# A fused attention and SoLU kernel: buffers named one by one, and a new order table

## The chip, the cores and the metric

The kernel runs on one core of a Trainium2 chip. The metric is the device time of one execution in microseconds (us). A core has five engines with queues of their own: TensorE (PE, matmuls), VectorE (DVE), ScalarE (ACT), GpSimd (POOL) and SyncE (SP). Each takes its instructions in the order of its queue. SP, ACT and POOL also issue DMA transfers.

## What is computed

```python
# q, k, v: (8, 8, 576, 64); x: (4608, 512); w_in: (512, 1024); w_out: (1024, 512)
kv = einsum('bhsd,bhse->bhde', k, v)
out = einsum('bhsd,bhde->bhse', q, kv)
out = out / sqrt(mean(out * out, -1) + 1e-6) * g_norm
x = out.transpose(0, 2, 1, 3).reshape(B * S, H * D)
h = x @ w_in
e = exp(h - max(h))
solu = h * e / (sum(e) + 1e-9)
ln = (solu - mean(solu)) / sqrt(var(solu) + 1e-6) * g_ln
return ln @ w_out
```

## The kernel before, in words

The 4608 tokens are nine tiles of 512 (c = 0 to 8). Tiles 0 to 7 take the first 512 tokens of a batch each; tile 8 takes the last 64 of all eight batches, and its q lies in a buffer of its own, q_last.

A tile goes through these pieces; a piece's name is its kind and its indices.

- `k.b`, `v.b`, `q.b`, `q_last.b` (lines 300 to 317): loads of a batch, DMAs that POOL issues, with a cast to bf16. `w_in`, `w_out` are loads of the weights, POOL's too.
- `kv_mm.b` (365): PE forms k^T v. `kv.b.x.part` (378): DVE or ACT copies it from PSUM.
- q is transposed: for tiles 0 to 3 by PE (`qT_mm`, 400) with a copy (`qT`), for tiles 4 to 8 by one transposing DMA that SP issues (`qT.c`, 411).
- `o_mm` (417) is q times kv; `sq`, `s_mm` or `s_pair`, `ln`, `ex` (430 to 462) make the root mean square of each head; `x` and `xc` (464 to 477) scale into x.
- `h.c.f` (520) is x times w_in for 128 of the 1024 columns; `exp.c.f` (527, ACT) is e; `u.c.f` (531, DVE) is h times e. No maximum is taken off and nothing is divided here; both go into the row factor below.
- `usq.c.f` (535, POOL or ACT) squares u; `es.c.n` (539, POOL) adds two of the e.
- `sums.c` (559, PE) adds u, usq and es over the columns with 80 small matmuls, in that order. `turn`, `stats` (DVE) and `rstd` (ACT) make of them one factor per token.
- `out.c.m.part` (618, PE) is u times the centred w_out; `ob.c.m` (633) scales it by rstd, on DVE or ACT; `store.c.m` (637) writes 128 rows with two DMAs from SP (tile 8: one DMA).

**What sets the order.** A class `Plan` (107) holds all pieces with what they need and which buffers they use. A table of words, `ORDER`, lists all 880 pieces once; `emit` (135) walks it and issues each piece on its engine (a suffix such as `:act` picks another). So each engine's queue is the table cut down to that engine. A second table, `HOME`, tells for some PSUM buffers in which group of banks they lie. Waits between engines are put in by the framework from the data and the buffers.

**Buffers.** PSUM has eight banks in the groups h (2), out (2), o (2), s, misc. SBUF buffers of a kind are kept in a number of slots (188 to 191): three for each of k, v, q and qT, four for e and ob, two for u, usq, es, x and wf. In the kernel before, `bank` (196) and `kept_tile` (202) ask the framework's pool for a tile with the kind's tag and that number of buffers, and the framework picks the slot when it places the tile. `emit` only asserts that the piece which takes a slot in turn comes behind all users of the tile that had it in turn. A load into a slot waits for the last reader of what was there.

A DMA that POOL or SP issues also takes one of eight semaphores of its side in turn, so it waits until the DMA eight issues earlier has landed.

Names of buffers in the profile: `misc_ps` in L372 is kv, in L405 q transposed, in L566 the sums; `qT_sb`, `q_sb`, `usq_sb`, `es_sb`, `u_sb`, `e_sb` are the tiles above; `wf_sb` holds w_out in 32 bits and later the scaled rows of odd tiles, `ob_sb` those of even tiles.

Of the kernel before, what the change touches and what calls it, by code (L numbers as in the profile page):

```python
# [20 lines left out]
warm load1.v load1.k v.0.0 k.0.0 v.0.1 g_in cast1.v:act q.0.0 k.0.1 q.0.1 q.1.0 cast1.k:act ident k.1.0 v.1.0 turn_g  # L21
kv_mm.0.0 warm.0 warm.2 kv.0.0.2 kv.0.0.1:act warm.1 kv.0.0.0:act qT_mm.0.0 warm.3 g_mean qT.0.0:act o_mm.0.0
kv_mm.0.1 sq.0.0.0 kv.0.1.2:act kv.0.1.0:act sq.0.0.1 w_in.1 kv.0.1.1 qT_mm.0.1 s_mm.0.0.0 warm.6 w_in.0 q.1.1 v.1.1
qT.0.1 k.1.1 s_mm.0.0.1 ex.0.0.1 x.0.0.1 o_mm.0.1 qT_mm.1.0 sq.0.1.1 qT.1.0 warm.5 w_out.0 sq.0.1.0 ex.0.0.0 w_out.1
s_mm.0.1.0 ex.0.1.0 s_mm.0.1.1 kv_mm.1.0 x.0.0.0 v.2.0 warm.4 kv.1.0.1 kv.1.0.0 ex.0.1.1 kv.1.0.2:act x.0.1.0 o_mm.1.0
table sq.1.0.0 h.0.5.0 x.0.1.1 sq.1.0.1 h.0.6.0 h.0.5.1 h.0.7.0 s_mm.1.0.1 h.0.7.1 h.0.1.0 exp.0.5 ln.1.0.1 exp.0.7
s_mm.1.0.0 u.0.5 h.0.1.1 h.0.6.1 ex.1.0.1 x.1.0.1 u.0.7 h.0.0.0 ln.1.0.0 qT_mm.1.1 h.0.3.0 qT.1.1 h.0.0.1 exp.0.1
h.0.2.0 h.0.3.1 kv_mm.1.1 ex.1.0.0 u.0.1 exp.0.6 h.0.2.1 exp.0.0 k.2.0 q.2.0 usq.0.7 q.3.0 exp.0.3 kv.1.1.2:act
kv.1.1.0:act exp.0.2 x.1.0.0 u.0.0 kv.1.1.1 o_mm.1.1 sq.1.1.1 h.0.4.0 u.0.6 h.1.0.0 s_mm.1.1.1 u.0.3 es.0.0 sq.1.1.0
u.0.2 ln.1.1.1 h.0.4.1 s_mm.1.1.0 ln.1.1.0 ex.1.1.0 ex.1.1.1 es.0.3 w_mean.0 x.1.1.0 h.1.5.0 es.0.1 v.3.0 usq.0.5  # L30
x.1.1.1 exp.0.4 es.0.2 w_mean.1 usq.0.1 usq.0.0:act u.0.4 h.1.2.0 w_center.4 h.1.6.0 h.1.0.1 usq.0.3:act w_center.2
exp.1.0 h.1.6.1 h.1.5.1 h.1.2.1 h.1.1.0 exp.1.6 exp.1.5 u.1.0 w_center.0 exp.1.2 u.1.5 k.3.0 h.1.7.0 h.1.1.1 u.1.6
k.4.0 exp.1.1 h.1.7.1 h.1.4.0 kv_mm.2.0 h.1.3.0 exp.1.7 kv.2.1.0:act kv.2.1.2:act kv.2.0.0:act kv.2.1.1:act h.1.4.1
q.4.0 v.4.0 usq.0.2 w_center.1 u.1.7 u.1.1 es.1.0 w_center.3 w_center.5 w_center.7 out.0.0.0 q_last.2 usq.0.4:act
w_center.6 kv.2.0.1:act out.0.3.0 h.1.3.1 kv.2.0.2:act exp.1.4 qT_mm.2.0 u.1.2 out.0.3.1 qT.2.0:act out.0.0.1
qT_mm.2.1 out.0.0.2 u.1.4 qT.2.1 o_mm.2.0 usq.0.6:act sums.0 turn.0 stats.0 out.0.0.3 exp.1.3 u.1.3 usq.1.1 sq.2.0.1
sq.2.0.0 out.0.3.2 usq.1.7 out.0.1.0 v.5.0 usq.1.2:act rstd.0 s_pair.2.0 ob.0.0 usq.1.0 k.5.0 ln.2.0.1 out.0.3.3
out.0.2.0 qT_mm.3.1 ob.0.3 ln.2.0.0 ex.2.0.1 o_mm.2.1 out.0.2.1 qT.3.1 sq.2.1.1 sq.2.1.0 es.1.3 usq.1.3 out.0.1.1
xc.2.0.1.0 out.0.2.2 xc.2.0.1.1 ex.2.0.0 usq.1.4 es.1.2 s_pair.2.1 out.0.1.2 ln.2.1.0 ln.2.1.1 store.0.0 out.0.2.3
out.0.1.3 ex.2.1.0 x.2.0.0 ob.0.2 ex.2.1.1 h.2.3.0 kv_mm.3.0 q.5.0 es.1.1 usq.1.5 ob.0.1:act store.0.3 qT.4 h.2.1.0  # L40
x.2.1.0 xc.2.1.1.1 store.0.2 kv.3.0.0:act h.2.7.0 h.2.6.0 h.2.0.0 xc.2.1.1.0 kv.3.1.1:act kv.3.1.2:act h.2.1.1 h.2.3.1
h.2.0.1 kv.3.0.1 kv.3.0.2 exp.2.1 qT_mm.3.0 h.2.7.1 kv.3.1.0 u.2.1 usq.1.6:act exp.2.3 exp.2.7 h.2.6.1 exp.2.0 exp.2.6
qT.3.0 h.2.4.0 sums.1 u.2.3 u.2.7 turn.1 k.6.0 v.6.0 u.2.0 o_mm.3.0 sq.3.0.1 h.2.4.1 out.1.3.0 stats.1 sq.3.0.0
exp.2.4 s_pair.3.0 h.2.5.0 out.1.3.1 ln.3.0.0 ex.3.0.0 u.2.4 qT.5 h.2.5.1 rstd.1 exp.2.5 u.2.6 x.3.0.0 ob.1.3 es.2.0
usq.2.1 u.2.5 out.1.0.0 kv_mm.4.0 kv.4.1.1 ln.3.0.1 h.2.2.0 o_mm.3.1 ex.3.0.1 kv.4.1.2:act h.2.2.1 out.1.0.1 kv.4.1.0
sq.3.1.0 xc.3.0.1.1 xc.3.0.1.0 ob.1.0 kv.4.0.0 sq.3.1.1 s_pair.3.1 out.1.1.0 usq.2.7 out.1.2.0 exp.2.2 ln.3.1.1
ex.3.1.1 q.6.0 u.2.2 es.2.2 k.7.0 ln.3.1.0 es.2.1 xc.3.1.1.1 usq.2.0 es.2.3 xc.3.1.1.0 ex.3.1.0 x.3.1.0 out.1.1.1
kv.4.0.1:act kv_mm.5.0 out.1.2.1 kv.5.0.0:act kv.4.0.2:act ob.1.1 h.3.2.1 h.3.0.1 kv.5.1.1 kv.5.1.0 h.3.1.1 usq.2.3
kv.5.1.2 exp.3.2 usq.2.6 u.3.2 usq.2.2:act usq.2.4:act h.3.5.1 ob.1.2 h.3.4.1 o_mm.4.1 usq.2.5 exp.3.0 u.3.0 kv.5.0.1
exp.3.1 exp.3.5 sq.4.1.0 es.3.0 u.3.1 sums.2 o_mm.4.0 kv.5.0.2 u.3.5 turn.2 stats.2 out.2.2.0 sq.4.1.1 store.0.1  # L50
store.1.1 exp.3.4 u.3.4 sq.4.0.1 s_pair.4.1 sq.4.0.0 out.2.2.1 usq.3.2 ln.4.1.1 ln.4.1.0 s_pair.4.0 ex.4.1.1 usq.3.0
xc.4.1.1.1 xc.4.1.1.0 es.3.2 ln.4.0.1 ex.4.0.1 ex.4.1.0 ln.4.0.0 xc.4.0.1.1 xc.4.0.1.0 rstd.2 out.2.0.0 x.4.1.0
out.2.0.1 h.3.7.1 store.1.3 kv_mm.6.0 ex.4.0.0 ob.2.0 usq.3.4:act h.3.3.1 out.2.3.0 kv.6.1.1 x.4.0.0 ob.2.2 h.3.6.1
exp.3.7 exp.3.3 out.2.3.1 usq.3.1 es.3.1 u.3.3 o_mm.5.0 exp.3.6 usq.3.3:act sq.5.0.1 u.3.7 usq.3.7 h.4.2.1 out.2.1.0
q_last.7 es.3.3 sq.5.0.0 kv.6.0.0 ob.2.3 kv.6.1.2 kv.6.0.2 kv.6.1.0 kv.6.0.1 s_pair.5.0 u.3.6 out.2.1.1 store.1.0
usq.3.5:act exp.4.2 h.4.1.1 ln.5.0.1 h.4.0.1 usq.3.6 ln.5.0.0 ex.5.0.1 v.7.0 q_last.1 u.4.2 ex.5.0.0 ob.2.1 exp.4.0
exp.4.1 h.4.4.1 sums.3 qT.6 xc.5.0.1.0 x.5.0.0 xc.5.0.1.1 u.4.0 o_mm.5.1 turn.3 exp.4.4 u.4.1 q_last.5 store.1.2
q_last.3 usq.4.0 q_last.4 q_last.6 usq.4.2 h.4.3.1 u.4.4 stats.3 sq.5.1.0 sq.5.1.1 h.4.5.1 s_pair.5.1 out.3.1.0
store.2.2 exp.4.3 ln.5.1.1 exp.4.5 rstd.3 u.4.3 u.4.5 h.4.7.1 ex.5.1.1 ln.5.1.0 out.3.1.1 h.4.6.1 out.3.0.0 kv_mm.7.0
ex.5.1.0 xc.5.1.1.0 xc.5.1.1.1 x.5.1.0 exp.4.7 o_mm.6.0 ob.3.1:act out.3.2.0 out.3.0.1 kv.7.0.0 kv.7.1.2 u.4.7  # L60
kv.7.1.1 store.2.1 usq.4.4 store.2.3 es.4.2 es.4.0 store.2.0 sq.6.0.0 kv.7.1.0:act sq.6.0.1 es.4.1 exp.4.6 kv.7.0.2
ob.3.0 u.4.6 usq.4.1 s_pair.6.0 kv.7.0.1:act out.3.2.1 usq.4.7 ln.6.0.0 ex.6.0.0 ln.6.0.1 h.5.5.1 exp.5.5 ob.3.2
ex.6.0.1 usq.4.3 usq.4.5 q.7.0 out.3.3.0 x.6.0.0 o_mm.6.1 sq.6.1.1 out.3.3.1 h.5.1.1 sq.6.1.0 es.4.3 s_pair.6.1
xc.6.0.1.1 xc.6.0.1.0 ln.6.1.0 exp.5.1 h.5.3.1 ob.3.3 u.5.5 u.5.1 exp.5.3 ex.6.1.0 out.4.1.0 usq.5.5 u.5.3 h.5.7.1
h.5.0.1 exp.5.7 ln.6.1.1 exp.5.0 x.6.1.0 h.5.4.1 qT.7 usq.4.6 u.5.7 u.5.0 usq.5.7 q_last.0 exp.5.4 h.5.2.1 ex.6.1.1
h.5.6.1 out.4.3.0 exp.5.2 u.5.2 u.5.4 sums.4 exp.5.6 usq.5.0:act es.5.2 u.5.6 usq.5.3 o_mm.7.0 turn.4 es.5.0 out.4.3.1
xc.6.1.1.1 stats.4 out.4.2.0 sq.7.0.1 sq.7.0.0 usq.5.1:act s_pair.7.0 out.4.2.1 out.4.1.1 rstd.4 ln.7.0.0 xc.6.1.1.0
ob.4.3 ln.7.0.1 ob.4.2 h.6.0.1 ex.7.0.0 x.7.0.0 out.4.0.0 h.6.6.1 out.4.0.1 h.6.5.1 usq.5.2 exp.6.0 ex.7.0.1
ob.4.1:act usq.5.6 es.5.3 xc.7.0.1.0 xc.7.0.1.1 usq.5.4 ob.4.0:act exp.6.6 qT.8 o_mm.7.1 sq.7.1.0 h.6.4.1 es.5.1 u.6.0
exp.6.5 sq.7.1.1 sums.5 usq.6.0 u.6.6 exp.6.4 u.6.5 turn.5 s_pair.7.1 ln.7.1.0 h.6.7.1 store.3.3 store.3.2 store.4.3  # L70
ln.7.1.1 ex.7.1.0 u.6.4 stats.5 x.7.1.0 h.6.3.1 h.6.2.1 h.6.1.1 exp.6.7 u.6.7 exp.6.3 out.5.0.0 u.6.3 out.5.1.0
usq.6.6 ex.7.1.1 exp.6.2 xc.7.1.1.1 u.6.2 usq.6.5 usq.6.3 exp.6.1 xc.7.1.1.0 u.6.1 out.5.2.0 o_mm.8.0 out.5.2.1
out.5.0.1 usq.6.7:act usq.6.2 usq.6.1 es.6.3 sq.8.0.1 sq.8.0.0 rstd.5 usq.6.4 store.3.1 store.4.1 s_pair.8.0 ln.8.0.1
ob.5.2 ln.8.0.0 es.6.0 out.5.1.1 out.5.3.0 h.7.6.1 ob.5.1 h.7.7.1 ob.5.0:act ex.8.0.1 h.7.1.1 ex.8.0.0 es.6.1
xc.8.0.1.1 xc.8.0.1.0 x.8.0.0 out.5.3.1 ob.5.3 exp.7.7 exp.7.1 store.4.2 store.4.0 store.5.2 exp.7.6 u.7.6 h.7.5.1
# [624 lines left out]
```

## Time and profile before

| what | value |
|---|---|
| three runs | 199.25, 200.31, 200.31 us; median 200.31 |
| profiled execution | 199.36 us, of which 197.5 us are the span from first to last instruction |
| mean granted TensorE clock | 0.977 |
| PE busy | 178.4 us (90%), 2227 matmuls |
| ACT busy | 144.8 us (73%) |
| POOL busy | 127.2 us (64%) |
| DVE busy | 125.6 us (64%) |
| DMA | 30.00 MB in 35420 packets |

How to read it: a row of the timeline gives start, duration, engine, line, operation, tile written and read, and in brackets how long the engine sat idle before it and what ended that. The rows of 40 digits cut the span into slices of 4.94 us, busy time in tenths; PEclk is the granted clock in tenths. The windows view gives, for each stretch, its length and then the busy time and number of instructions of each engine, the granted clock, the DMA engines' share and rate. The chain of waits of this execution goes back from the last store through PE alone, with hardly a wait, as far as it is shown (148 us). The trace also gives the time at which each load landed.

### The profile page before, as it was taken

How to read it: one execution, taken by the hardware profiler on the slowest of the kernel's cores; microseconds unless marked ns; L12 is line 12 of the kernel's file. 1: busy time of each engine (PE TensorE's matmuls, PEld its weight loads, DVE VectorE, ACT ScalarE, POOL GpSimd, SP SyncE). 2: the span in 40 equal slices, each digit the busy share in tenths (PEclk: the TensorE clock that was granted, in tenths of full speed). 3: DMA queues.
4: the chain of work that ended last, by engine and by line, in shares of the span. 5: the costliest groups of instructions: out<-in, count | busy, mean ns of one | idle time of the engine just before them, and what ended most of it. 6: DMA issues, size and time to landing. Idle time of an engine off the chain costs nothing. (4 is left out here: it accounts for less than half of the span.)

```text
span 197.5 us, 5401 instructions
## 1 busy us (share of the span) xinstructions
PE 178.4 (90%) x2227; PEld 85.1 (43%) x2227; DVE 125.6 (64%) x247; ACT 144.8 (73%) x255; POOL 127.2 (64%) x136
## 2 busy tenths in 40 slices
PE   7668999999999998179999999999999999999990
...
PEclk9999999999999999859999999999999999999997
...
GB/s 157 177 205 206 206 389 229 207 209 209 235 218 199 158 172 221 246 244 133 10 60 114 234 7 84 129 63 209 145 80 29 188 3 0 65 201 3 23 242 165
DMA packets 35420, 30.00 MB, mean 152 GB/s; under 512 B 16316, under 2 KB 29636, under 8 KB 35396
## 3 DMA queue, kind: packets, MB, share of 16 engines
...
q10 hardware_dynamic: 576, 0.92, 1.3%
...
## 5 line engine op out<-in xcount | busy, mean ns | idle before, releaser
L620 PE MATMUL out_ps<-w_out_sb,u_sb 128*128 128x512 bf16 x288 | 70.1, 384 | 0.1
L522 PE MATMUL h_ps<-x_sb,w_in_sb 128*128 128x512 bf16 x288 | 69.3, 380 | 0.3 <-DVE x_sb L466 0.2
L216 POOL TENSOR_TENSOR usq_sb<-u_sb 128x512 bf16<-128x512 bf16 x50 | 51.2, 1038 | 14.7 <-DVE u_sb L533 14.5
L533 DVE TENSOR_TENSOR u_sb<-h_ps,e_sb 128x512 bf16<-128x512 f32 x72 | 47.4, 685 | 17.2 <-ACT e_sb L529 16.0
L541 POOL TENSOR_TENSOR es_sb<-e_sb 128x512 bf16<-128x512 f32 x36 | 45.5, 1274 | 19.2 <-ACT e_sb L529 14.2
L529 ACT ACTIVATE e_sb<-h_ps,zero_t 128x512 f32<-128x512 f32 x72 | 46.3, 689 | 15.3 <-PE h_ps L522 11.7
L522 PEld LDWEIGHTS <-w_in_sb 128*128 128x128 bf16 x288 | 26.8, 97 | 33.6 <-issue 4.2
L620 PEld LDWEIGHTS <-u_sb 128*128 128x128 bf16 x288 | 26.6, 98 | 33.6 <-issue 4.7
L214 ACT ACTIVATE osq_sb<-o_ps,zero_t 128x512 bf16<-128x512 f32 x36 | 23.2, 685 | 9.4 <-PE o_ps L424 9.2
L474 DVE SCALAR_TENSOR_TENSOR x_sb<-o_ps,g_cols,rst_sb 64x512 bf16<-64x512 f32 x28 | 21.0, 750 | 7.4 <-ACT rst_sb L454 6.9
L450 ACT ACTIVATE lss_sb<-s_ps,eps_t 128x512 f32<-128x512 f32 x32 | 21.0, 682 | 3.0 <-PE s_ps L443 2.9
L454 ACT ACTIVATE rst_sb<-lss_sb,zero_t 128x512 f32<-128x512 f32 x32 | 22.6, 722 | 0.4
L466 DVE SCALAR_TENSOR_TENSOR x_sb<-o_ps,g_cols,rst_sb 128x512 bf16<-128x512 f32 x22 | 16.3, 749 | 8.4 <-ACT rst_sb L454 6.5
L305 POOL DMA_DIRECT2D q_sb<-in_q_dram x10 | 7.6, 764 | 15.5 <-DMA qT_sb<-q_sb 13.1
L214 ACT ACTIVATE usq_sb<-u_sb,zero_t 128x512 bf16<-128x512 bf16 x22 | 15.1, 718 | 0.8 <-DVE u_sb L533 0.8
L566 PEld LDWEIGHTS <-stat_sel 128*32 128x32 bf16 x720 | 10.6, 99 | 9.9 <-issue 9.5
L222 DVE TENSOR_SCALAR wf_sb<-out_ps,rstd 128x512 f32<-128x512 f32 x13 | 9.7, 745 | 7.2 <-PE out_ps L620 4.7
L566 PE MATMUL misc_ps<-usq_sb,stat_sel 128*32 128x128 bf16 x288 | 6.2, 225 | 6.5 <-POOL usq_sb L216 6.5
L210 DVE CAST kvd<-misc_ps 64x128 bf16<-64x128 f32 (+1 forms) x15 | 4.3, 287 | 11.8 <-PE misc_ps L372 6.7
L222 DVE TENSOR_SCALAR ob_sb<-out_ps,rstd 128x512 f32<-128x512 f32 (+1 forms) x13 | 9.1, 727 | 2.3 <-ACT ob_sb L220 1.8
L573 DVE STREAM_TRANSPOSE misc_ps<-misc_ps 128x128 f32<-128x128 f32 x9 | 3.0, 328 | 11.4 <-PE misc_ps L566 10.4
L424 PE MATMUL o_ps<-qT_sb,kvd 64*64 64x256 bf16 (+1 forms) x192 | 8.7, 258 | 1.2 <-ACT qT_sb L210 0.7
...
## 6 DMA issues: line engine op xcount, KB each, us to landing
...
```

The costliest lines, as they stand in the source:

```text
L214: nc.scalar.activation(out=dst, in_=src, func=AF.Square, bias=zero_t[:, :])
L216: on[engine].tensor_tensor(out=dst, in0=src, in1=src, op=MUL)
L222: nc.vector.tensor_scalar_mul(out=dst, in0=src, scalar1=by)
L450: nc.scalar.activation(out=t[:, :], in_=T["s", i][:, :], func=AF.Ln, bias=eps_t[:, :])
L454: nc.scalar.activation(out=t.rearrange("p a b c -> p (a b c)"), in_=T["lss", i][:, :], func=AF.Exp, scale=-0.5, bias=zero_t[:, :])
L474: nc.vector.scalar_tensor_tensor(out=t[rows, 2 * hf:2 * hf + 2, 1], in0=T["o", c, hf, 1][rows, :, :, :], scalar=g_cols[rows, NF:NF + 1], i ...
L522: nc.tensor.matmul(bank(("h", c, f), [128, 512])[:, :], w_in_sb[:, dt, f * 128:(f + 1) * 128], T["x", c][:, dt].rearrange("p a b c -> p (a ...
L529: nc.scalar.activation(out=t[:, f % 2, :], in_=T["h", c, f][:, :], func=AF.Exp, bias=zero_t[:, :])
L533: nc.vector.tensor_tensor(out=t[:, f, :], in0=T["h", c, f][:, :], in1=T["e", c, f // 2][:, f % 2, :], op=MUL)
L541: on[engine].tensor_tensor(out=t[:, n, :], in0=e[:, 0, :], in1=e[:, 1, :], op=ADD)
L566: nc.tensor.matmul(t[32 * j:32 * j + 32, 0, :], stat_sel[:, i, :], cols, start=(part == 0 and n == 0), stop=(part == 2 and n == n_src - 1) ...
L620: nc.tensor.matmul(bank(("out", c, m), [128, d_model])[:, :], T["u", c][:, f, m * 128:(m + 1) * 128], w_out_sb[:, f, :], start=(f == 0), s ...
```

## The change

Three things change, and nothing else: no piece is added or left out.

1. **Slots.** Every slot is a tag of its own (`q0`, `q1`, `q2`), and `emit` picks it: a free list per kind, filled when the last user of a tile has been issued, and taken from at the front. So a new tile takes the slot whose last user stands earliest in the table.
2. **ORDER** is another order of the same 880 pieces, and some pieces change engine (25 instead of 22 of the kv copies on ACT, 21 instead of 22 of the usq, 13 instead of 11 of the scalings).
3. **HOME** is another table of PSUM groups.

```diff
     def __init__(self, slots):
-        self.pieces, self.users, self.slots, self.homes = {}, {}, slots, {}
+        self.pieces, self.users, self.slots, self.homes, self.place = {}, {}, slots, {}, {}
...
-        done, held = set(), {tag: [] for tag in self.slots}
+        done, left = set(), {key: len(names) for key, names in self.users.items()}
+        free = {tag: ["%s%d" % (tag, i) for i in range(n)] for tag, n in self.slots.items()}
...
             for key in uses:
-                tag = self.home(key)
-                if key not in held[tag]:
-                    held[tag].append(key)
-                    if len(held[tag]) > self.slots[tag]:
-                        old = held[tag][-1 - self.slots[tag]]
-                        assert done.issuperset(self.users[old]), (name, old)
+                if key not in self.place:
+                    self.place[key] = free[self.home(key)].pop(0)
+                left[key] -= 1
+            for key in uses:
+                if not left[key]:
+                    free[self.home(key)].append(self.place[key])
...
-            tag = plan.home(key)
-            T[key] = ps.tile(shape, dtype, name=key[0] + "_ps", tag=tag, bufs=banks[tag])
+            T[key] = ps.tile(shape, dtype, name=key[0] + "_ps", tag=plan.place[key])
...
-            T[key] = sb.tile(shape, dtype, name=key[0] + "_sb", tag=key[0], bufs=kept[key[0]])
+            T[key] = sb.tile(shape, dtype, name=key[0] + "_sb", tag=plan.place[key])
```

Of the order, POOL's part between the sums of tiles 0 and 3 (loads of k, v, q and q_last among the es and usq pieces), the table before:

```
usq.1.1 usq.1.7 v.5.0 usq.1.0 k.5.0 es.1.3 usq.1.3 usq.1.4 es.1.2 q.5.0 es.1.1 usq.1.5 k.6.0 v.6.0
es.2.0 usq.2.1 usq.2.7 q.6.0 es.2.2 k.7.0 es.2.1 usq.2.0 es.2.3 usq.2.3 usq.2.6 usq.2.5
es.3.0 [sums.2] usq.3.2 usq.3.0 es.3.2 usq.3.1 es.3.1 usq.3.7 q_last.7 es.3.3 usq.3.6 v.7.0 q_last.1 [sums.3]
```

and after:

```
es.1.3 k.5.0 usq.1.1 usq.1.0 usq.1.7 q.5.0 es.1.1 es.1.0 es.1.2 usq.1.3 usq.1.4 usq.1.2
usq.2.0 es.2.0 usq.2.1 es.2.2 q_last.4 es.2.3 q_last.2 usq.2.6 es.2.1 usq.2.4 usq.2.7 usq.2.3
v.6.0 [sums.2] k.6.0 es.3.0 usq.3.5 q.6.0 es.3.2 usq.3.0 usq.3.2 usq.3.1 q_last.0 usq.3.4 q_last.6 es.3.1
usq.3.6 v.7.0 es.3.3 usq.3.3 [sums.3] k.7.0 q_last.1 usq.4.0 q_last.3 q_last.7 q_last.5 usq.4.1 q.7.0
```

On SP, qT.4 stands behind two stores of tile 0 in the table before and ahead of all stores after; the stores of tiles 0 to 2 stand later among the transposes. At the end, sums.8 stands ahead of nine parts of out before and of five after.

More of the change, by code (lines that the diff above doesn't have):

```diff
@@ L20 @@
 ORDER = """
[L21 to L75, printed above, removed]
@@ L76 @@
-h.7.0.1 h.7.3.1 es.6.2 exp.7.3 h.7.4.1 es.7.3 u.7.1 u.7.7 sums.6 u.7.3 exp.7.0 exp.7.4 exp.7.5 o_mm.8.1 u.7.5 h.7.2.1
-sq.8.1.1 exp.7.2 store.3.0 sq.8.1.0 u.7.4 turn.6 out.6.2.0 out.6.3.0 stats.6 s_pair.8.1 u.7.2 u.7.0 out.6.1.0
-usq.7.1:act ln.8.1.1 ln.8.1.0 out.6.3.1 store.5.0 es.7.0 usq.7.5 es.7.2 out.6.1.1 usq.7.6 usq.7.7 usq.7.3 ex.8.1.0
-ex.8.1.1 out.6.0.0 store.5.1 x.8.1.0 out.6.2.1 xc.8.1.1.1 xc.8.1.1.0 rstd.6 out.6.0.1 h.8.2.1 ob.6.1:act h.8.4.1
-ob.6.3 ob.6.2 h.8.3.1 h.8.0.1 usq.7.2 ob.6.0 exp.8.3 h.8.6.1 exp.8.2 exp.8.4 es.7.1 h.8.1.1 u.8.3 exp.8.6 u.8.2 u.8.4
@@ L81 @@
-usq.8.2:act h.8.5.1 exp.8.0 exp.8.1 h.8.7.1 exp.8.5 u.8.0 exp.8.7 es.8.1 out.7.1.0 out.7.2.0 u.8.1 store.6.2 u.8.5
-u.8.6 store.6.1 store.5.3 usq.8.6:act usq.8.1:act out.7.0.0 es.8.0 out.7.2.1 out.7.1.1 es.8.2 usq.8.4 usq.8.3:act
-usq.7.4:act usq.8.5 u.8.7 usq.8.0 out.8.2.0 usq.7.0:act out.7.0.1 store.6.3 sums.7 usq.8.7:act es.8.3 sums.8 turn.7
-stats.7 rstd.7 store.6.0 ob.7.2 turn.8 out.8.2.1 out.8.3.0 ob.7.0:act out.7.3.0 ob.7.1 store.7.0 stats.8 store.7.2
-store.7.1 out.8.1.0 out.8.0.0 out.8.1.1 rstd.8 ob.8.2:act store.8.2:act out.7.3.1 ob.7.3 out.8.0.1 ob.8.1:act
@@ L86 @@
-out.8.3.1 store.8.1:act store.7.3 ob.8.0:act store.8.0:act ob.8.3.1:act ob.8.3.0 store.8.3.0 store.8.3.1:act
+warm load1.k load1.v g_in k.0.0 v.0.0 v.0.1 cast1.v q.0.0 k.0.1 q.0.1 q.1.0 ident turn_g warm.0 cast1.k:act k.1.0
+kv_mm.0.0 kv.0.0.2:act warm.2 qT_mm.0.0 v.1.0 warm.3 g_mean kv.0.0.0:act kv_mm.0.1 kv.0.0.1:act qT.0.0:act o_mm.0.0
+kv.0.1.0:act w_in.1 w_in.0 q.1.1 v.1.1 k.1.1 qT_mm.0.1 sq.0.0.0 sq.0.0.1 w_out.0 kv.0.1.1 kv.0.1.2 qT.0.1 s_mm.0.0.0
+warm.6 s_mm.0.0.1 ex.0.0.0 ex.0.0.1 o_mm.0.1 qT_mm.1.0 sq.0.1.1 warm.5 x.0.0.0 sq.0.1.0 qT.1.0 s_mm.0.1.0 s_mm.0.1.1
@@ new lines @@
+x.0.0.1 warm.4 w_out.1 v.2.0 k.2.0 kv_mm.1.0 ex.0.1.1 ex.0.1.0 kv.1.0.2:act kv.1.0.1 warm.1 kv.1.0.0 table o_mm.1.0
+h.0.5.0 x.0.1.0 x.0.1.1 sq.1.0.0 h.0.6.0 h.0.5.1 h.0.7.0 sq.1.0.1 exp.0.5 s_mm.1.0.1 ln.1.0.1 h.0.7.1 s_mm.1.0.0
+h.0.1.0 h.0.6.1 u.0.5 h.0.0.0 h.0.1.1 ln.1.0.0 h.0.0.1 ex.1.0.1 q.2.0 usq.0.5 x.1.0.1 v.3.0 q.3.0 exp.0.7 u.0.7
+ex.1.0.0 h.0.3.0 qT_mm.1.1 h.0.3.1 h.0.2.0 kv_mm.1.1 x.1.0.0 exp.0.0 exp.0.1 u.0.0 exp.0.6 exp.0.3 qT.1.1 u.0.1
+kv.1.1.1 kv.1.1.0:act u.0.6 kv.1.1.2:act h.0.2.1 exp.0.2 o_mm.1.1 sq.1.1.1 sq.1.1.0 h.0.4.0 u.0.3 h.1.0.0 es.0.0 u.0.2
@@ new lines @@
+s_mm.1.1.1 ln.1.1.1 h.0.4.1 s_mm.1.1.0 ln.1.1.0 h.1.5.0 w_mean.0 ex.1.1.0 ex.1.1.1 x.1.1.0 exp.0.4 x.1.1.1 w_mean.1
+u.0.4 usq.0.0 h.1.2.0 h.1.0.1 h.1.5.1 h.1.1.0 exp.1.0 h.1.6.0 h.1.1.1 h.1.6.1 q.4.0 usq.0.3 es.0.3 usq.0.7 w_center.4
+h.1.2.1 es.0.1 exp.1.5 exp.1.6 exp.1.1 u.1.0 w_center.0 usq.0.2 k.3.0 es.0.2 usq.0.6 exp.1.2 h.1.7.0 u.1.5 h.1.4.0
+w_center.1 u.1.6 h.1.7.1 kv_mm.2.0 u.1.1 w_center.2 h.1.3.0 h.1.4.1 h.1.3.1 exp.1.7 kv.2.0.0:act u.1.7 kv.2.1.0:act
+k.4.0 w_center.3 w_center.5 w_center.7 u.1.2 w_center.6 out.0.3.0 usq.0.1:act kv.2.1.2:act kv.2.1.1:act exp.1.4
@@ new lines @@
+out.0.0.0 out.0.3.1 kv.2.0.1:act qT_mm.2.0 usq.0.4 v.4.0 usq.1.5 v.5.0 kv.2.0.2:act qT.2.0:act out.0.3.2 sums.0 turn.0
+es.1.3 o_mm.2.0 k.5.0 usq.1.1 usq.1.0 stats.0 exp.1.3 out.0.0.1 out.0.3.3 out.0.0.2 sq.2.0.1 sq.2.0.0 rstd.0
+s_pair.2.0 out.0.0.3 ln.2.0.0 usq.1.7 u.1.4 u.1.3 ob.0.3 qT_mm.2.1 q.5.0 ln.2.0.1 ex.2.0.0 qT_mm.3.1 qT.2.1 out.0.1.0
+ex.2.0.1 ob.0.0 qT.3.1 o_mm.2.1 out.0.1.1 es.1.1 es.1.0 es.1.2 usq.1.3 out.0.2.0 out.0.1.2 out.0.2.1 x.2.0.0 sq.2.1.0
+sq.2.1.1 s_pair.2.1 ln.2.1.1 out.0.1.3 usq.1.4 out.0.2.2 xc.2.0.1.0 ln.2.1.0 usq.1.2 xc.2.0.1.1 h.2.0.0 ob.0.1 h.2.3.0
@@ new lines @@
+ex.2.1.1 xc.2.1.1.1 xc.2.1.1.0 out.0.2.3 kv_mm.3.0 qT_mm.3.0 ex.2.1.0 ob.0.2:act h.2.7.0 kv.3.1.1:act x.2.1.0 kv.3.1.0
+h.2.1.0 h.2.3.1 h.2.7.1 usq.1.6:act h.2.1.1 exp.2.3 h.2.0.1 exp.2.7 exp.2.1 kv.3.0.1:act kv.3.1.2 kv.3.0.2
+kv.3.0.0:act h.2.4.0 qT.3.0 u.2.3 u.2.1 u.2.7 h.2.6.0 h.2.4.1 h.2.6.1 exp.2.4 u.2.4 sums.1 exp.2.0 o_mm.3.0 turn.1
+h.2.5.0 stats.1 exp.2.6 sq.3.0.0 sq.3.0.1 out.1.3.0 h.2.5.1 u.2.6 s_pair.3.0 u.2.0 rstd.1 exp.2.5 ln.3.0.0 out.1.2.0
+ln.3.0.1 out.1.3.1 usq.2.0 u.2.5 es.2.0 qT.4 ex.3.0.0 ob.1.3 o_mm.3.1 kv_mm.4.0 kv.4.0.0 h.2.2.0 out.1.2.1 sq.3.1.1
@@ new lines @@
+sq.3.1.0 kv.4.1.2:act kv.4.1.0:act usq.2.1 es.2.2 store.0.3 ex.3.0.1 q_last.4 store.0.1 kv.4.0.2 kv.4.0.1 kv.4.1.1
+x.3.0.0 store.0.0 s_pair.3.1 ln.3.1.0 h.2.2.1 xc.3.0.1.1 ex.3.1.0 ln.3.1.1 x.3.1.0 xc.3.0.1.0 out.1.0.0 es.2.3
+ex.3.1.1 q_last.2 out.1.0.1 out.1.1.0 kv_mm.5.0 usq.2.6 xc.3.1.1.0 exp.2.2 xc.3.1.1.1 es.2.1 ob.1.2:act usq.2.4
+usq.2.7 kv.5.0.1:act usq.2.3 ob.1.0 u.2.2 out.1.1.1 usq.2.5:act ob.1.1:act kv.5.1.0:act kv.5.1.2:act h.3.2.1 h.3.0.1
+kv.5.1.1 o_mm.4.0 h.3.4.1 exp.3.2 kv.5.0.0 exp.3.0 u.3.2 kv.5.0.2 usq.2.2:act sq.4.0.1 v.6.0 u.3.0 h.3.1.1 h.3.5.1
@@ new lines @@
+exp.3.4 exp.3.1 exp.3.5 sq.4.0.0 u.3.1 u.3.5 sums.2 k.6.0 es.3.0 usq.3.5 q.6.0 o_mm.4.1 u.3.4 turn.2 stats.2 sq.4.1.1
+out.2.0.0 sq.4.1.0 out.2.2.0 rstd.2 s_pair.4.1 out.2.2.1 ln.4.1.0 ln.4.1.1 ex.4.1.1 ex.4.1.0 ob.2.2 out.2.0.1
+store.1.0 qT.5 xc.4.1.1.0 s_pair.4.0 ln.4.0.1 out.2.3.0 es.3.2 x.4.1.0 ln.4.0.0 out.2.3.1 xc.4.1.1.1 h.3.3.1 ex.4.0.1
+h.3.6.1 ex.4.0.0 ob.2.0:act usq.3.0 usq.3.2 exp.3.3 h.3.7.1 kv_mm.6.0 usq.3.1 ob.2.3:act exp.3.6 kv.6.0.2:act
+kv.6.0.1:act xc.4.0.1.0 xc.4.0.1.1 x.4.0.0 q_last.0 u.3.3 u.3.6 kv.6.1.2 o_mm.5.0 exp.3.7 u.3.7 kv.6.0.0 out.2.1.0
@@ new lines @@
+kv.6.1.1 usq.3.4 q_last.6 h.4.2.1 out.2.1.1 es.3.1 usq.3.6 sq.5.0.1 sq.5.0.0 v.7.0 es.3.3 usq.3.3 store.2.3 s_pair.5.0
+h.4.0.1 ob.2.1 usq.3.7:act exp.4.2 h.4.4.1 ln.5.0.1 u.4.2 qT.6 ex.5.0.1 kv.6.1.0 ln.5.0.0 h.4.1.1 ex.5.0.0 exp.4.0
+xc.5.0.1.1 xc.5.0.1.0 x.5.0.0 exp.4.1 exp.4.4 sums.3 u.4.0 store.0.2 u.4.1 u.4.4 o_mm.5.1 turn.3 h.4.5.1 k.7.0
+q_last.1 store.2.2 usq.4.0 q_last.3 q_last.7 q_last.5 usq.4.1 q.7.0 sq.5.1.1 store.2.0 stats.3 h.4.3.1 sq.5.1.0
+exp.4.5 out.3.1.0 s_pair.5.1 out.3.0.0 exp.4.3 rstd.3 ln.5.1.1 ex.5.1.1 u.4.5 out.3.1.1 u.4.3 ln.5.1.0 xc.5.1.1.0
```

53 lines of the change are left out of this document (40 added, 13 removed).

## The prediction

> **What bounds the kernel now.** I read the page first: PE is busy 90% of the span, no other engine over 73%, and every slice but a few has nine tenths. So the question is where PE is not at work, or not at its clock.
>
> ```profile
> PE   7668999999999998179999999999999999999990
> ...
> PEclk9999999999999999859999999999999999999997
> ```
>
> Two places: the first four slices, and slices 17 to 19 (79 to 94 us), where PE sits idle and then runs at a lower granted clock. The windows view gives that second place its size.
>
> ```profile
> core 0: us, PE busy (x) PEld busy (x) DVE busy (x) ACT busy (x) POOL busy (x), PEclk, DMA share, GB/s
> 20.00:77.40 57.40, 56.62 (x787) 27.78 (x780) 44.92 (x82) 49.75 (x91) 35.37 (x37) 1.00 1.25 222
> 77.40:94.50 17.10, 10.04 (x172) 4.50 (x171) 7.32 (x16) 9.96 (x18) 13.27 (x13) 0.80 1.01 198
> 94.50:148.00 53.50, 53.01 (x623) 24.19 (x612) 42.66 (x80) 45.93 (x80) 40.04 (x40) 1.00 0.62 105
> 148.00:193.50 45.50, 44.55 (x493) 21.53 (x492) 24.00 (x48) 29.04 (x51) 25.50 (x23) 1.00 0.35 85
> ```
>
> PE fills 56.62 of 57.40, 53.01 of 53.50 and 44.55 of 45.50 us of the other stretches: there is nothing to win there but about 2 us. The timeline of PE shows what happens at 77.4: the sums of tile 2 (L566) start, their first 32 matmuls read u, and then they wait three times for POOL's squares.
>
> ```profile
> 77.42 0.63 PE L566 MATMUL misc_ps<-u_sb,stat_sel 128*32 128x128 bf16 x32
> 81.10 0.35 PE L566 MATMUL misc_ps<-usq_sb,stat_sel 128*32 128x128 bf16 x12 [3.05 <-POOL usq_sb L216]
> 83.31 0.41 PE L566 MATMUL misc_ps<-usq_sb,stat_sel 128*32 128x128 bf16 x8 [1.86 <-POOL usq_sb L216]
> 85.30 0.51 PE L566 MATMUL misc_ps<-usq_sb,stat_sel 128*32 128x128 bf16 x12 [1.59 <-POOL usq_sb L216]
> ```
>
> Why is POOL late? Its timeline and SP's:
>
> ```profile
> 60.76 2.02 POOL L216 TENSOR_TENSOR usq_sb<-u_sb 128x512 bf16<-128x512 bf16 x2
> 75.93 0.80 POOL L305 DMA_DIRECT2D q_sb<-in_q_dram  x1 [13.14 <-DMA qT_sb<-q_sb]
> 76.75 1.28 POOL L541 TENSOR_TENSOR es_sb<-e_sb 128x512 bf16<-128x512 f32 x1
> ```
>
> ```profile
> 54.64 8.17 SPq L413 DMA_TRANSPOSE qT_sb<-q_sb  x1
> ```
>
> POOL stands 13.14 us before the load of q.6, which waits for the transpose qT.4 (issued 54.64, landed 75.39 by the trace's landing times: 20.75 us). In the built program before, q.6 takes the buffer of q.4, whose only reader is that transpose, although the buffer of q.3 came free when PE's last transpose of it ended at 57.6. Behind q.6 in POOL's queue stand seven of the ten es and usq pieces that POOL does for tile 2.
>
> **What the stall costs.** From 77.42 (sums.2) to 94.08 (kv_mm.6.0) PE does sums.2 1.23 (the same group at 104.74 to 105.97), one o_mm 0.34, 20 matmuls 128x512 at 0.2165 (32 of them take 6.91 to 7.03 us on the chain) = 4.33, and two s_pair at 0.34: 6.6 us of work in 16.66 us. The loss is **10.1 us**: 6.5 of waits for POOL, and 3.6 of small waits behind it and of the half clock (out_ps x4 at 86.74 takes 1.89 us against 1.04 elsewhere).
>
> [...]
>
> **The change, part by part.**
>
> *Slots.* No instruction is added. In the built program after, q.6 takes q.3's buffer and waits only for the landing of v.4. The wait on a transpose moves to q.7, which takes q.4's buffer and comes some 19 us later than q.6; qT.4 is long done. Gain: the 10.1 us, if tile 2's pieces are then in time. Other buffers that change: ob.2.1 takes that of ob.2.3 and waits for store.2.3 to land (issue 1.2 us, landing 3.2: about 2 us of DVE waiting near 91 us). Behind it stands u.4.2, which itself needs exp.4.2 at that time: price 0, up to 0.7.
>
> *Order: the same pieces on PE* (167.3 us of matmul work in both tables by the rows above), so only waits can differ. I add the PE work that stands ahead of a piece in the table, and take PE's clock as that work plus 12.55 us, its lateness at sums.2 before (64.87 us ahead, start 77.42; 10.5 at sums.0). POOL pieces cost 1.0 (usq), 1.24 (es), 0.8 (DMA issue), from stretches like 164.26 4.03 x4 and 27.92 3.73 x3. The tight places:
> - *Start.* w_in.1 lands at 19.86 and the first h starts at 20.11; its place in POOL's queue is the same. 0.
> - *sums.0, sums.1.* POOL begins es.0.0 near 27.5 (exp.0.1 is the fourth exp on ACT) and has nothing to wait for: 13 us of tile 0 end near 40.6, sums.0 comes at 32.45 + 10.5 = 42.9; tile 1 ends near 56, sums.1 comes at 47.5 + 11.7 = 59.2. 0, margins 2 to 3 us.
> - *sums.2.* Its last es needs exp.2.2, which stands on ACT behind two ln and two ex (2.6 us) that follow s_pair.3.1 (55.24 + 12.3 = 67.6): 71.0. Then es 1.24 and three usq 3.0: 75.3. The usq part of sums.2 comes at 77.42 + 0.46. Margin 2.5 us: 0.
> - *kv_mm.6.0* needs v.6 and k.6, which now stand behind those pieces: issued 75.3 and 76.1, where before they were issued at 54.4 and 55.2. PE comes to it at 74.94 + 12.55 = 87.5. Nearest rows for such a landing: 8.2 us (q.6, issued 75.93) and 11.4 (k.7, second of its pair, 77.97 to 89.34), farther 6.9 (v.7) and 20.0 and 23.2 (k.6 and v.6 before, behind a full queue). I take k.7's: landed 87.5, price 0.1; ends 0 and 12 of waiting.
> - *sums.3.* Seven usq, four es and six DMA issues from 75.3: 16.8 us, done 92.1; sums.3 at 81.52 + 12.55 = 94.1. 0, margin 2.
> - *SP.* qT.4 now is first in SP's queue and starts when q.4 lands (about 48); even with 20.75 us it lands at 69 and o_mm.4.0 comes at 74.5. qT.5 follows store.1.0 (about 73.5); with qT.6's 7.05 us it lands at 80.6, o_mm.5.0 comes at 88.2. 0. The loads share the DMA engines with qT.4 earlier: k.3 lands near 52 instead of 48.3, kv_mm.3.0 comes at 53.5. 0, margin 1.5.
> - *End.* Five parts of out (4.33 us) stand behind sums.8 instead of nine. The chain turn, stats, rstd took 184.82 to 188.17 = 3.35 us; with two scalings on DVE after it (1.45) it ends 0.5 us after PE, beside the last two halves on ACT (1.0). 0, up to +0.5.
>
> Sum, against the profiled execution (199.36, span 197.5): 199.36 - 10.1 + 0.1 = 189.4. The median shown is 200.31, 0.95 above that execution; I add half: **190.0**. Of this case alone 187.8 (the 2 us elsewhere shrink) to 191.5 (k.6 later by 2 us).
>
> **Rivals.**
> - *The other engines want the pause back* (192 to 197). ACT is busy 87% of 20 to 77.4 and 58% of the stalled 17.1 us. Squeezed into 7 us, its 9.96 us of work put it 3 us behind; with 13% spare it needs 20 us and more to catch up. If PE waits for that, 189.4 + 3 = 192.4; if POOL's margins of 2 us break as well, each at 2 us, up to 197. For it: the margins are small. Against it: ACT at 87% held PE at 99% before 77.4.
> - *Slower: the late loads of v.6 and k.6.* One mechanism: they stand behind usq.2.3 on POOL. If they take the 20.0 and 23.2 us of before, k.6 lands at 96 to 99, PE idles 9 to 12 us and pays once more the 3.6 us that came on top of the waits here: 189.4 + 12.6 to 15.6 = 202 to 205. It decides from an idle time of 6.4 us, a landing 18 us after the issue. For it: those rows are these very loads. Against it: then eight loads were queued; at 75 the queue is empty but for qT.5. [...]
> - *The change does nothing for PE* (about 199.5): the stall moves to another load that waits for a transpose, at the same price. The built program shows only q.7, issued 20 us after qT.4's end, so this is unlikely.
>
> **Chances.** Forecast 0.64, pause wanted back 0.21, late loads 0.10, nothing 0.05. About 0.5% is what a measurement can tell here. Faster 0.64 + 0.21 = 0.85, same 0.05, slower 0.10. The range 187.8 to 197.0 leaves out the last two and a little of each end.
>
> **What would show it.** Right: no POOL row waits for qT_sb over 1 us; PE's sums wait for usq under 1 us; granted clock 1.00 from 20 us to the end; PE end near 182.5. k.6 decides kv_mm.6.0: a wait of L372 for k_sb is the third step gone wrong. Wrong altogether: a new low slice in PE's row with a low clock behind it.

## The result, and the profile after

The changed kernel takes 193.0 us (median of four executions, 192.28 to 194.36), the kernel before 200.31 beside it; the ratio is 0.964 (95% interval 0.955 to 0.972). Once more, in a later run: 192.79 against 200.04, 0.965 (0.962 to 0.967). Ratios are of undisturbed executions, so where some were disturbed the median of all lies a little above what the ratio gives, and the profiles of runs e3, e4 and e10, disturbed ones, are not read. The forecast was 190.0, the range 187.8 to 197.0.

The profiled execution took 193.26 us, its span 191.5. First the two rows of slices:

```profile
PE   7777989997996999999999699999999999999990
...
PEclk9999999999999999999999999999999999999999
```

The kernel before had a hole in slices 17 to 19; it is gone and the clock stays up. Single low slices are new: the 10th (43 to 48 us), the 13th (57 to 62) and the 23rd (105 to 110). The windows:

```profile
core 0: us, PE busy (x) PEld busy (x) DVE busy (x) ACT busy (x) POOL busy (x), PEclk, DMA share, GB/s
20.00:77.40 57.40, 53.08 (x762) 26.56 (x769) 43.67 (x79) 48.03 (x90) 44.49 (x45) 1.00 1.12 204
77.40:94.50 17.10, 16.77 (x239) 7.73 (x239) 12.35 (x25) 16.25 (x30) 15.86 (x17) 1.00 1.09 173
94.50:148.00 53.50, 50.72 (x593) 23.66 (x598) 40.32 (x74) 45.89 (x80) 36.66 (x37) 1.00 0.75 144
```

In the middle window PE's busy time goes from 10.04 to 16.77 us and the clock from 0.80 to 1.00: that is the gain. In the windows around it PE has lost some (56.62 to 53.08, 53.01 to 50.72). Not all of that is idle: this trace lacks 23 of the 2227 matmuls. So the losses are read from the waits, not from these sums. The timelines of PE, POOL and SP at the old place:

```profile
79.49 0.63 PE L566 MATMUL misc_ps<-u_sb,stat_sel 128*32 128x128 bf16 x32
79.95 0.62 PE L566 MATMUL misc_ps<-usq_sb,stat_sel 128*32 128x128 bf16 x32
80.39 0.40 PE L566 MATMUL misc_ps<-es_sb,stat_sel 128*32 128x128 bf16 x16
```

```profile
74.75 3.03 POOL L216 TENSOR_TENSOR usq_sb<-u_sb 128x512 bf16<-128x512 bf16 x3
77.72 0.81 POOL L305 DMA_DIRECT2D v_sb<-in_v_dram  x1
78.52 0.75 POOL L305 DMA_DIRECT2D k_sb<-in_k_dram  x1
...
82.14 0.80 POOL L305 DMA_DIRECT2D q_sb<-in_q_dram  x1
```

```profile
48.25 8.22 SPq L413 DMA_TRANSPOSE qT_sb<-q_sb  x1
```

No row here has the bracket that tells of idle time: sums.2 runs without a wait, and POOL does not wait before q.6 (82.14). POOL's tile 2 work ends at 77.7, and all three loads come behind it. qT.4 is issued at 48.25 and lands at 68.65 (20.40 us), 13 us before q.6 is issued.

PE comes to sums.2 at 79.49, which is 2.1 us later than before. The list of PE's waits has the reason, and a second one for what follows:

```profile
PE misc_ps L372 <- DMA k_sb<-in_k_dram: 2.3, 2, 1.9
PE h_ps L522 <- DVE qT_sb L210: 1.6, 1, 1.6
```

The columns are the sum, the number of waits and the longest. Second line first, with the rows of PE and DVE:

```profile
59.69 1.46 PE L522 MATMUL h_ps<-x_sb,w_in_sb 128*128 128x512 bf16 x6 [1.58 <-DVE qT_sb L210]
```

```profile
58.63 0.28 DVE L210 CAST kvd<-misc_ps 64x128 bf16<-64x128 f32 x1 [2.40 <-ACT kvd L210]
58.95 0.69 DVE L210 COPY qT_sb<-misc_ps 128x1024 bf16<-128x1024 bf16 x1
```

h.2.6.0 takes the PSUM bank that held the transpose qT.3.0. That bank is emptied by a copy on DVE, which stands behind kv.3.0.2; and kv.3.0.2 waits 2.40 us for ACT's kv.3.0.1. PE pays 1.58 us for it. The other wait, from PE's timeline, and the load behind it, from the chain of waits:

```profile
107.16 0.22 PE L372 MATMUL misc_ps<-v_sb,k_sb 64*64 64x64 bf16 x2 [1.92 <-DMA k_sb<-in_k_dram]
```

```profile
95.67 11.44 DMA k_sb<-in_k_dram
```

This is k.7, issued at 95.67 behind qT.6 (91.98 to 100.68) and v.7 (92.64 to 102.43) and landed at 107.11. PE wanted it at 105.24 (107.16 less the wait of 1.92).

### The profile page after: what moved, and what is told of

Its sections match the earlier page's. It is cut to its first block, busy times and chain, and to the rows that moved or that the text cites. A ratio compares the mean times of both kernels' runs of the same rounds, so it can differ in the third digit from the quotient of the medians.

```text
span 191.5 us, 5359 instructions
## 1 busy us (share of the span) xinstructions
PE 173.8 (91%) x2204; PEld 83.6 (44%) x2227; DVE 124.6 (65%) x243; ACT 145.8 (76%) x258; POOL 128.4 (67%) x137
## 4 chain that ended last, share of the span: by engine, by line
PE 58%; ACT 10%; DMA 10%; POOL 9%; DVE 7%; issue 4%; DVEq 0%; POOLq 0%; ACTq 0%
PE out_ps L620 24%; PE h_ps L522 21%; DMA k_sb<-in_k_dram 10%; PE misc_ps L566 5%; POOL usq_sb L216 4%; POOL es_sb L541 3%; PE o_ps L424 3%; ACT e_sb L529 3%; DVE u_sb L533 2%; ACT osq_sb L214 2%; PE s_ps L443 2%; DVE x_sb L466 2%; ACT rst_sb L454 2%; ACT rst_sb L460 1%; PE misc_ps L372 1%
## 5 line engine op out<-in xcount | busy, mean ns | idle before, releaser
L522 PE MATMUL h_ps<-x_sb,w_in_sb 128*128 128x512 bf16 x277 | 67.9, 379 | 2.6 <-DVE qT_sb L210 1.6
L620 PE MATMUL out_ps<-w_out_sb,u_sb 128*128 128x512 bf16 x279 | 66.7, 379 | 1.4 <-issue 1.1
L216 POOL TENSOR_TENSOR usq_sb<-u_sb 128x512 bf16<-128x512 bf16 x51 | 52.3, 1038 | 20.8 <-DVE u_sb L533 20.6
L522 PEld LDWEIGHTS <-w_in_sb 128*128 128x128 bf16 x288 | 26.7, 98 | 35.2 <-issue 6.2
L222 DVE TENSOR_SCALAR ob_sb<-out_ps,rstd 128x512 f32<-128x512 f32 x14 | 10.1, 748 | 5.1 <-PE out_ps L620 3.6
L281 PE MATMUL s_ps<-zeros 128*128 128x512 bf16 x23 | 8.8, 511 | 1.6 <-DVE zero_t L240 1.2
L222 DVE TENSOR_SCALAR wf_sb<-out_ps,rstd 128x512 f32<-128x512 f32 x10 | 7.3, 749 | 3.8 <-PE out_ps L620 1.9
L372 PE MATMUL misc_ps<-v_sb,k_sb 64*64 64x64 bf16 x360 | 7.6, 194 | 2.3 <-DMA k_sb<-in_k_dram 2.3
L305 POOL DMA_DIRECT2D k_sb<-in_k_dram x10 | 7.6, 757 | 2.9 <-DMA w_in_sb<-in_moe_w_in_dram 1.5
```

Source lines behind the costliest of these rows:

```text
L216: on[engine].tensor_tensor(out=dst, in0=src, in1=src, op=MUL)
L522: nc.tensor.matmul(bank(("h", c, f), [128, 512])[:, :], w_in_sb[:, dt, f * 128:(f + 1) * 128], T["x", c][:, dt].rearrange("p a b c -> p (a ...
L620: nc.tensor.matmul(bank(("out", c, m), [128, d_model])[:, :], T["u", c][:, f, m * 128:(m + 1) * 128], w_out_sb[:, f, :], start=(f == 0), s ...
```

## The experiments

**What made the gain: the slots or the order?** The first two runs exchange the slot rule and the two tables (ORDER and HOME, moved together here). Run e1 has the code of the changed kernel with the two tables of before (in short, for the tables are long):

```diff
-ORDER, HOME of the changed kernel
+ORDER, HOME of the kernel before
```

> The slot rule of the change with the order table and bank table of before. Theory A (the gain comes from the order): in this table qT.4 stands ahead of the last transpose of q.3, so the rule, too, gives q.6 the buffer of q.4; POOL waits some 13 us for qT_sb, PE some 6.5 us in the sums of tile 2, and the time is that of before, 199 to 201 us. Theory B (the prediction's reading: the rule takes the wait away): 189 to 191 us, no such wait.

Measured: 203.28 us against 199.89, ratio 1.018 (1.014 to 1.023). The rule alone does not help; it is 1.8% slower. POOL and PE of e1:

```profile
79.61 0.80 POOL L305 DMA_DIRECT2D q_sb<-in_q_dram  x1 [16.42 <-DMA qT_sb<-q_sb]
```

```profile
84.76 0.51 PE L566 MATMUL misc_ps<-usq_sb,stat_sel 128*32 128x128 bf16 x12 [4.67 <-POOL usq_sb L216]
86.97 0.40 PE L566 MATMUL misc_ps<-usq_sb,stat_sel 128*32 128x128 bf16 x8 [1.70 <-POOL usq_sb L216]
88.96 0.51 PE L566 MATMUL misc_ps<-usq_sb,stat_sel 128*32 128x128 bf16 x12 [1.59 <-POOL usq_sb L216]
```

The same stall, 16.42 us instead of 13.14. In the old table the last reader of q.3 (qT_mm.3.0, on PE) stands *behind* qT.4, the last reader of q.4. "Earliest last user" therefore gives q.6 the buffer of q.4, as the framework did. Position in a table is not time: qT_mm.3.0 ends at 57.6 in the profile of before, qT.4 lands at 75.39. Why e1's wait is 3.3 us longer: its profile has q.4 landing at 56.27 instead of 54.57 and qT.4 taking 22.73 us instead of 20.75. What brings these about in e1, which differs from before only in the slots that the rule picks, stayed open.

Run e2 has the tables of the changed kernel with the framework's slots:

```diff
-            T[key] = sb.tile(shape, dtype, name=key[0] + "_sb", tag=plan.place[key])
+            T[key] = sb.tile(shape, dtype, name=key[0] + "_sb", tag=key[0], bufs=kept[key[0]])
```

> The order table and bank table of the change, slots picked by the framework as before. Here the framework gives q.6 the buffer of q.4. Theory A: the load of q.6 stands so late in POOL's queue (issued near 82 us) that the transpose qT.4 (landed near 69) is long done, so nothing waits: 192 to 194.5 us, as the changed kernel. Theory B: the wait on a transpose is back and the time is 199 us or more.

Measured: 192.43 us, ratio 0.962 (0.960 to 0.965): the whole gain. Here q.6 takes the buffer of q.4, the very choice that stalls POOL in the old order, and POOL does not wait before it, since the load is issued at 81.45 and qT.4 has landed at 67.86:

```profile
81.45 0.81 POOL L306 DMA_DIRECT2D q_sb<-in_q_dram  x1
```

**Is the stall that one wait?** Run e5 is e1 with one choice changed: q.6 takes the second of the free list, the buffer of q.3.

```diff
-                    self.place[key] = free[self.home(key)].pop(0)
+                    self.place[key] = free[self.home(key)].pop(1 if key == ("q", 6) else 0)
```

> The kernel of before with one buffer changed by hand: q.6 takes the buffer of q.3 (and q.7 that of q.4). Order, banks and every other buffer of the rule-alone kernel stay. If the wait of q.6 on qT.4 is the whole cause of the stall at the sums of tile 2: PE gains the 10.1 us that the prediction worked out, 189.0 to 190.5 us, granted clock 1.00. Rival (the other engines want the pause back, or POOL is late for another reason): 192 to 197 us, with waits of PE for usq or e behind the sums of tile 2.

Measured: 190.31 us, ratio 0.952 (0.949 to 0.954); 13 us below e1 from one choice of buffer, and below the changed kernel. POOL's row and the slices of e5:

```profile
62.37 0.80 POOL L305 DMA_DIRECT2D q_sb<-in_q_dram  x1
```

```profile
PE   7777899999999999989999999999999999999990
...
PEclk9999999999999999999999999999999999999997
```

Run e9 does the same in the kernel before itself, with the framework's slots for everything but q:

```diff
+            if key[0] == "q":
+                T[key] = sb.tile(shape, dtype, name="q_sb", tag="q%d" % (0, 1, 2, 0, 1, 2, 0, 1)[key[1]], bufs=1)
+            else:
-            T[key] = sb.tile(shape, dtype, name=key[0] + "_sb", tag=key[0], bufs=kept[key[0]])
+                T[key] = sb.tile(shape, dtype, name=key[0] + "_sb", tag=key[0], bufs=kept[key[0]])
```

> The kernel before in everything (order, table of PSUM groups, the framework's choice of every other slot) but the buffers of q: q.6 takes that of q.3 and q.7 that of q.4. Theory A (the wait of q.6 for qT.4 is the whole loss): 189.4 to 190.5 us, as the run with the rule's other slots and this one buffer. Theory B (the other slots of the rule cost 3 us in the old order, as the rule alone came out 3.4 us slower): 186.5 to 188 us.

Measured: 190.81 us, ratio 0.954 (0.950 to 0.958). No gain or loss from the other slots shows once the wait is gone (e5: 0.952); theory B is out.

Run e3 leaves the buffer and moves the load, in the kernel before, behind POOL's squares of tile 2 (here and below the fences show only the words around the place):

```diff
-ex.3.1.1 q.6.0 u.2.2
+ex.3.1.1 u.2.2
...
-usq.2.5 exp.3.0
+usq.2.5 q.6.0 exp.3.0
```

> The kernel before with one word moved: the load q.6 stands behind the squares of tile 2 (behind usq.2.5) instead of ahead of them; the buffers are those of before, so q.6 still takes the one of q.4 and still waits for the transposing DMA qT.4. Theory A (what costs the time is POOL's work queued behind the waiting load, the buffer alone costs nothing): the wait goes or shrinks below 3 us, PE's wait for the squares in sums.2 goes, the clock stays at 1.00, and the time is 190 to 193 us. Theory B (the buffer itself costs, since q.6 comes late in any case): q.6 and k.6 land late, a wait of L372 or of the transposing DMA qT.6 takes the place, 195 us and more.

Measured: 190.40 to 194.37 us in four executions (median 192.73), ratio 0.956 (0.950 to 0.961), level with e9's 0.954. So the buffer itself costs nothing that these runs can tell; what costs is the work queued behind a load that waits. There are two cures, another buffer (e5, e9) or another place (e3). The changed kernel has both, and by e1 and e2 it is the second, from its order, that makes its gain.

**What keeps the changed kernel at 193?** Run e6 moves one word in it: the copy qT.3.0 goes ahead of the kv copies on DVE.

```diff
-kv.3.0.1:act kv.3.1.2 kv.3.0.2
-kv.3.0.0:act h.2.4.0 qT.3.0 u.2.3
+kv.3.0.1:act qT.3.0 kv.3.1.2 kv.3.0.2
+kv.3.0.0:act h.2.4.0 u.2.3
```

> The changed kernel with one word moved: DVE's copy qT.3.0 stands ahead of the two kv copies kv.3.1.2 and kv.3.0.2, which wait for ACT. Theory A (PE's idle 1.6 us ahead of h.2.6.0 come from DVE's queue and are added to the end): the wait of L522 for qT_sb goes, and the time is 1.2 to 1.7 us below the changed kernel, 191.3 to 191.8 us. Theory B (PE is made to wait for something else a little later, the loads k.6 and k.7 above all, which come at their own time): the loads' waits grow by the same, and the time stays at 192.5 to 193 us.

Measured: 191.35 us, ratio 0.957 (0.953 to 0.961). PE's wait of L522 for qT_sb is gone from its list, which now begins:

```profile
PE misc_ps L372 <- DMA k_sb<-in_k_dram: 1.8, 2, 1.4
PE misc_ps L405 <- DMA q_sb<-in_q_dram: 1.3, 2, 0.9
```

The next two go for k.7. Run e4 issues it right behind v.7, some 2 us earlier:

```diff
-v.7.0 es.3.3
+v.7.0 k.7.0 es.3.3
...
-h.4.5.1 k.7.0
+h.4.5.1
```

> The changed kernel with the load of k.7 moved on POOL from behind the sums of tile 3 to right behind v.7, ahead of one es and one usq piece: issued near 93.4 instead of 95.7 us. If the 2.07 us by which PE falls behind at kv_mm.7.0 are the landing of k.7 (107.1, needed at 105.1): the wait shrinks to 0 or a few tenths, 191 to 191.7 us against 193.0. Rival: the landing does not come earlier, since the transpose qT.6 and v.7 share the DMA engines: 193, the wait stays at 1.5 to 2 us.

Measured: 193.61 us, ratio 0.967 (0.963 to 0.971): no gain over the changed kernel (0.965). The time is the rival's of the expectation; whether k.7 landed earlier is not shown. Run e7 issues v.7 10 us and k.7 12 us earlier, behind q.6 and ahead of qT.6:

```diff
-q.6.0 o_mm.4.1
+q.6.0 v.7.0 k.7.0 o_mm.4.1
```

> The changed kernel with two words moved: the loads v.7 and k.7 stand right behind q.6, some 10 and 13 us earlier, ahead of the transposing DMA qT.6 instead of behind it. Theory A (k.7 comes late because it is issued late and behind qT.6): k.7 lands near 97 to 100 us, PE's wait of L372 of 1.9 us goes, qT.6 takes longer without harm, 190.8 to 191.5 us. Theory B (the DMA engines have no room there, and something else is late, qT.6 or q_last): another wait takes the place, 193 us and more.

Measured: 195.17 us, ratio 0.976 (0.970 to 0.982), slower than the changed kernel. k.7 landed at 98.00, in good time, and no wait of L372 for k is left. A new one took its place, on DVE and then on PE:

```profile
96.48 0.75 DVE L222 TENSOR_SCALAR ob_sb<-out_ps,rstd 128x512 f32<-128x512 f32 x1 [3.58 <-DMA out_dram<-ob_sb]
```

```profile
97.29 3.32 PE L522 MATMUL h_ps<-x_sb,w_in_sb 128*128 128x512 bf16 x8 [2.66 <-DVE ob_sb L222]
```

This is ob.2.1, which takes the slot of ob.2.3 and waits for store.2.3. With v.7 and k.7 on the DMA engines that store's two transfers (issued 89.78 and 90.29) took 5.5 and 6.1 us, where they take 2.9 and 3.0 in the changed kernel. There the second lands at 93.78 and ob.2.1, which also needs PE's out.2.1, starts at 93.87: the store came only 0.09 us ahead of it.

Run e10 is e7 with a third word moved, the store of ob.0.2 from behind u.4.0 to behind store.0.0. The rule then gives ob.2.1 the slot of ob.0.2 instead of that of ob.2.3.

```diff
-x.3.0.0 store.0.0 s_pair.3.1
+x.3.0.0 store.0.0 store.0.2 s_pair.3.1
```

> The changed kernel with v.7 and k.7 behind q.6 (as in the run before, which came out at 195.2 us) and a third word moved: store.0.2 stands behind store.0.0, so that the slot of ob.0.2 is free early, and ob.2.1 takes it instead of that of ob.2.3. Theory A (the early loads gain what they should, and it was the scaling ob.2.1, waiting in DVE's queue 3.58 us for store.2.3, that ate it): no wait of DVE for a store, PE's 2.7 us of waiting for it gone, no wait of L372, 190.8 to 191.7 us. Theory B (the DMA engines have no room there): the store's wait comes back as a wait for the transposing DMA qT.6 or for a load, 193 us and more.

Measured: 191.01 us, ratio 0.956 (0.954 to 0.959). Four us below e7, the time of theory A; that the wait for the store is gone is read from e11, which has the same three moves. Run e11 adds the word of e6:

> The same and qT.3.0 ahead of the two kv copies on DVE. Theory A (the three losses of the changed kernel's middle add up: 1.7 for h.2.6.0, 1.9 for k.7): 189.0 to 190.0 us, level with or a little below the old order with q.6 in q.3's buffer. Theory B (the loads and transposing DMAs come at their own time, so a gain in one place is a wait in the next): 191 us and more.

Measured: 189.42 us (189.14 to 190.28), ratio 0.948 (0.946 to 0.951). No wait in PE's list is over 1.2 us, and neither k_sb of L372 nor qT_sb of L522 is among the first:

```profile
PE s_ps L281 <- DVE zero_t L240: 1.2, 1, 1.2
PE out_ps L620 <- issue: 1.1, 7, 0.2
PE misc_ps L405 <- DMA q_sb<-in_q_dram: 1.0, 2, 0.7
```

The first transfer of store.2.3 still takes 5.9 us (issued 88.37, landed 94.31), but ob.2.1 no longer needs it and starts at 91.96, released by PE:

```profile
91.96 0.75 DVE L222 TENSOR_SCALAR ob_sb<-out_ps,rstd 128x512 f32<-128x512 f32 x1 [0.46 <-PE out_ps L620]
```

Two repeats stood beside it, the changed kernel (e12) and e5 (e13):

> The changed kernel once more, to stand beside the others on one chip: 192.5 to 193.5 us; PE's waits of 1.6 us for qT_sb and 1 to 2 us for k_sb are there again if they belong to the kernel and not to one execution.

> The old order with the rule's slots but q.6 in the buffer of q.3, once more, to stand beside the others on one chip: 190 to 190.7 us, 2 to 3 us below the changed kernel.

Measured: 192.79 us for the changed kernel, again with 1.6 us of waiting for qT_sb, and with 2.8 for k_sb where 1 to 2 had been expected, and 190.71 for e5 (ratio 0.954, 0.952 to 0.956). So e11, four words from the changed kernel, is the fastest of all: 3.4 us below it and 1.3 below e5.

## Why the prediction was right and where it failed

**The size of the loss** was nearly right. The prediction put it at 10.1 us; taking only this stall out of the kernel before is worth 9.0 us in e9 (199.77 to 190.81), 9.6 in e5 and 9.3 in its repeat.

**The cause was not.** The step "Slots" put the gain down to the rule: "q.6 takes q.3's buffer". True of the changed kernel's layout, but it decides nothing there (e2), and in the old order the rule does not make that choice (e1). The gain belongs to the order (with its table of banks), which puts POOL's tile 2 work ahead of v.6, k.6 and q.6. The buffers of both programs were compared, but the rule was never worked out on the old table. Three of the signs that the prediction asked for (no wait of POOL for qT_sb, none of the sums for usq, the clock at 1.00) came true, and none of them can tell a rule from an order. The fourth, PE's end near 182.5, did not: it came at 186.7.

**PE's lateness** was the first of two steps that made the number 3 us too low. I took the 12.55 us at sums.2 over to the new order; there it is 79.49 - 64.87 = 14.6. Of the 2.1 us, the wait of h.2.6.0 is 1.6. Another 0.9 stand inside sums.0 with no releaser named in the trace (0.4 to 1.1 in other runs of this order; its cause is open). An earlier start gives 0.4 back (sums.0 starts at 42.5, not 42.9). I followed POOL, SP and the loads through the new order, but not DVE, whose queue decided when the bank of qT.3.0 came free (1.58 us of PE's waiting), and not the new table of banks that made h.2.6.0 need that copy.

**k.7**, the second step, was left out. The text named a wait of L372 for k_sb as the sign of a wrong third step, but worked it out for k.6 alone. k.6 was right: issued 78.52, landed 89.41, 10.9 us by the row of 11.4, and PE came at 90.12. k.7 takes 11.44 as that row says, but is issued only at 95.67: 1.9 us of waiting. The two terms, 2.1 and 2.1 (the lateness that PE gains at kv_mm.7.0), are the 4.2 us between PE's predicted end (182.5) and its end here (182.18 + 4.49 = 186.7); and taking both waits out (e11) brings 189.4.

**The other tight places** held: tile 2's squares came at 77.7 (predicted 75.3) and sums.2 just behind, qT.4 landed at 68.65 (69), k.3 at 50.96 (52), qT.5 took 7.93 us (7.05), sums.1 and sums.3 did not wait, and after PE's end come 4.8 us, as before. For ob.2.1 the price "0, up to 0.7" was right by luck, with a store that landed 0.09 us ahead: e7 shows the same wait at 3.58 on DVE and 2.66 on PE.

**The rivals.** The measured 193.0 lies above the 187.8 to 191.5 that the prediction gave for its own case, and in the band of "the other engines want the pause back" (192 to 197). That the whole range holds it is luck, for that mechanism does not show: ACT fills 16.25 of the 17.10 us and PE runs on beside it, and what PE waits for is a DVE copy at 59.7, ahead of the old pause, and a load. Of the 9 to 12 us that the rival of the late loads feared, 1.9 came, and for k.7 rather than k.6. Loads ahead of other transfers did hold them up in e7: with POOL's v.7 and k.7 ahead of them, the two transfers of SP's store.2.3 took 5.5 and 6.1 us, against 2.9 and 3.0 in the changed kernel.
